# Phi moved to VectorE, a sine table to ScalarE, and a new order of the plan, in a gated mix of memory attention and a spectral filter

## The chip, the cores and the metric

One core of a Trainium2 chip runs the whole kernel in one launch. The metric is the device time of the program in microseconds, from 2048 tokens of width 640 in HBM to the output in HBM. The engines are TensorE (PE in the profile), VectorE (DVE), ScalarE (ACT), GpSimd (POOL) and SyncE (SP), which here only issues transfers.

## The reference

Two branches work on inputs of 2048 x 640 in bf16, and a gate per token mixes them. Branch A is attention with a compressive memory in 4 segments of 512 tokens, with 32 heads of width 20. Both branches get `A_x` as their x; `B_x` is not used.

```python
g = sigmoid((x * gate_w).sum(-1))
# A, for each segment s of 4, each head
phi = lambda t: where(t > 0, t + 1.0, exp(t))
p     = softmax(qs @ ks.T * 20**-0.5 + causal_mask)
a_dot = p @ vs
a_mem = (phi(qs) @ M) / (phi(qs) @ z + 1e-6)
o     = sigmoid(beta) * a_mem + (1 - sigmoid(beta)) * a_dot
M, z  = M + phi(ks).T @ vs, z + phi(ks).sum(0)
a     = concat(o) @ wo
# B
b = irfft2(rfft2(x) * (w_r + 1j * w_i))
out = g * a + (1 - g) * b
```

## The kernel before

The kernel is written as a graph of operations. `Graph.op` records each operation with the engine or the engines that may run it, what it reads and writes, a duration in the planner's own units of microseconds (`dur`) and a priority (`pr`; the lower value goes first). `Graph.schedule` then lays all operations out in time by these durations: at each step it takes, among what is ready, the operation that could start first, and by priority where several could start within 0.04 us. An operation that needs PSUM takes one of eight banks when it starts (`acq`) and gives it back with the copy that empties it (`rel`); `AHEAD` says how far in priority an operation may run ahead of the most urgent one that still needs a bank of its class. Where an operation may run on two engines, as the copies out of PSUM may on ScalarE and VectorE, the plan chooses one. `Emit` writes the instructions of each engine in the planned order, with semaphore waits between the engines. On the chip each engine then goes through its list in this fixed order; the durations in the plan no longer matter there.

The planner also imitates TensorE's clock: where it sees TensorE idle before an operation, it may put dummy matmuls there (L495), each of 512 columns, which read only `xT` and write to the bank that the operation has just been given. `WARM` holds the time from which this is done, a lower and an upper bound for the share of recent TensorE work, and the largest number of dummies in one place. `Emit.emit` writes the waits of an operation first, and then the operation's instructions, the dummies at their head.

The set-up (`tables`) computes arguments on VectorE and sines on ScalarE, for cosine and sine tables: `Df` for the transform along the width, `tab0` to `tab5` for the transform along the tokens, `Di` for the way back. The odd sine table `tab3` is made from the odd cosine table `tab2`, read backwards and multiplied with a sign for each partition (`scol`); before, this is a GpSimd instruction of 2048 columns (L822). All exponentials of the kernel are ordered behind all sines, so that ScalarE changes its function table once.

The spectral branch folds `xT` by symmetry on VectorE, multiplies with `Df` into `Z`, transforms along the tokens (`Aev`, `Bev`), filters with the weights `W` (`filter`: `X1`, `X2`, `Mt`, `Nt`, `St`, results in `FG`) and transforms back into `YT`; its start is spread by `DF0`, `DF1`, `FWD0`, `FWD1`, `INV0`, `INV1`.

The attention goes over 32 slots: 4 segments with 8 groups of 4 heads. For each 128 tokens `project` makes k, q and v (`pk`, `nq`, `vaug`), stores k and q to HBM on SP's queue (`hk`, `hq`), and computes phi of both in place; phi of q is stored too (`hp`). `fetch` reads them back transposed (`kT`, `qT`, `pqT`), also on SP's queue. `scores` multiplies them, takes the exponential on ScalarE (`ex`) and clears the upper triangle of the diagonal blocks on GpSimd (`affine_select`, L1144); `weigh` multiplies with `vaug` and with the memory `Mz`, and normalizes on VectorE. `memory_update` adds phi(k) times v. `project_out` makes 128 rows of the output: the last step of the spectral branch (`cs`, `ys`; the two additions into `ys` may run on GpSimd or VectorE), the transposes of `osb`, the product with `wo`, and the sum on VectorE (`outt`, L1215).

Phi is the part that the change touches most. Before, it is computed as max(t, 0) + min(exp(t), 1), with the exponential on ScalarE, both limits on GpSimd (L1068 and L1069) and the sum on VectorE. It runs 24 times (12 for k and 12 for q, over 128 x 640 each), and there is one buffer `ek` for the exponential, so that one phi ends before the next begins. The instructions of the helpers `ve`, `tt`, `act`, `copy` and `po` appear in the profile with the helpers' lines: L535 is a VectorE operation on two tensors, L514 a ScalarE function, L525 and L528 are copies on ScalarE and VectorE, and L497 is a matmul.

Of the kernel before, what the change touches and what calls it, by code (L numbers as in the profile page):

```python
# [6 lines left out]
ACT = mybir.ActivationFunctionType  # L7
ALU = mybir.AluOpType
# [425 lines left out]

UNITS = ((0,), (1, 3), (2,))

DF0, DF1, FWD0, FWD1, INV0, INV1, PR0, PR1 = -15.079, 0.53, -3.827, 1.2, 8.0, 0.819, -16.0, 0.105

GATE, OUT0, OUT1, YLEAD = -16.128, (14.574, 23.59, 27.761, 32.159), 0.707, 0.204

PC0, PC1 = 0.3, 0.562
NOSB = 2
NCS = 2

YENG = ("pool", "dve")

TRP, DIP = -15.053, -29.071

WARM = (24.0, 0.437, 0.837, 6)

SC0, SCP, SCU, WG0, WG1, FE0, FE1 = 0.0, 0.359, 0.076, 1.221, -0.212, 0.125, -0.026
AHEAD = 1.4


EXU = {(0,): (0, 512), (1, 3): (1024, 512), (2,): (2048, 256)}
# [11 lines left out]
class Kern(Graph):  # L467
# [40 lines left out]
            return h  # L508
        return self.op("pe", fn, r=list(r) + [self.ident.keys[0]], w=[req], dur=0.06 * n, pr=pr, acq=req if acq else None)

    def act(self, out, in_, func, r, w, n, pr, scale=1.0, bias=None, rel=None):
        def fn(e):
            kw = {} if bias is None else {"bias": bias}
            return e.activation(out(), in_(), func, scale=scale, **kw)  # L514
        o = self.op("act", fn, r=r, w=w, dur=0.05 + n * 0.000835, pr=pr, rel=rel)
        if func == ACT.Sin:
            self.sins.append(o)
        if func == ACT.Exp:
            o.after.update(self.sins)
        return o  # L520
# [160 lines left out]
    def loads(self):  # L681
        x2 = self.x2
        for i, c in enumerate((0, 3, 1, 2)):
            self.dma("sp", self.xT[:, :, c * L:(c + 1) * L], x2[c * L:(c + 1) * L, :], [], [self.xT.keys[c]], lat=4.0, transpose=True, dur=4.2, pr=-100 + i)
        self.dma("act", self.gwrow[0:5, :], self.gate_w.rearrange("(t p) -> t p", p=P), [], [self.gwrow.keys[0]], lat=3.0)
        self.dma("act", self.beta[:, :], AP(self.A_beta.tensor, self.A_beta.offset, [[0, P], [1, H]]), [], [self.beta.keys[0]], lat=3.0)
        for i, j in enumerate((1, 0, 2)):
            t, w = self.wqkv[j], (self.A_wq, self.A_wk, self.A_wv)[j]
            self.dma("act", t[:, :, :], w.rearrange("(t p) e -> p t e", p=P), [], [t.keys[0]], lat=8.0 + 2.5 * i, pr=-99 + i, dur=0.5)

        self.late = []
        for t in range(4):
            self.load_w(0, t)
        self.late.append(self.dma("sp", self.wo[:, :, :], self.A_wo.rearrange("(t p) e -> p t e", p=P), [], [self.wo.keys[0]], lat=6.0, pr=0, dur=0.5))
# [83 lines left out]
    def tables(self):  # L778
        k = lambda t: t.keys[0]
        n = [0]  # L780

        def make(dst, wkeys, prods, rk, width, mask, scale, pr, parts=None):
            a = self.arg[n[0] % 2]
            n[0] += 1
            for (o, row, c, ph, cost) in prods:
                out = a.ap(o[0], o[1])
                self.op("dve", lambda e, out=out, row=row, c=c, ph=ph: e.tensor_scalar(out, row, c, ph, ALU.mult, ALU.add), r=rk, w=[k(a)], dur=0.07 + cost * 0.00065, pr=pr)  # L787
            self.ve(lambda e: e.tensor_scalar(a[:, 0:width], a[:, 0:width], mask, None, ALU.bitwise_and), [k(a)], [k(a)], width, pr, rate=1.6)  # L788
            for (d_, off, dims) in (parts or [(dst, 0, [[1, width]])]):
                self.act(lambda d_=d_: d_, lambda off=off, dims=dims: a.ap(off, dims), ACT.Sin, [k(a), k(self.npi)], wkeys, width, pr, scale=scale, bias=self.npi[:, 0:1])  # L790

        dsc = 2 * PI / 65536.0
        ssc = 2 * PI / 4096.0
        dc, cf = self.dcol, self.colf

        for (t0, nt) in ((0, 3), (3, 2)):
            pr = []
            for t in range(t0, t0 + nt):
                for j, ph in ((0, 49152.0), (1, 0.0)):
                    pr.append((((t - t0) * 2 * HC + j * HC, [[1, HC]]), self.krow[:, :], dc[:, t:t + 1], ph, HC))  # L800
            make(self.Df.ap(t0 * 2 * HC, [[1, nt * 2 * HC]]), [k(self.Df)], pr, [k(self.krow), k(dc)], nt * 2 * HC, 65535, dsc, -40)
        self.ve(lambda e: e.memset(self.Df.ap(HC + 319, [[2 * HC, 5], [1, 2]]), 0.0), [], [k(self.Df)], 10, -40)
        er, orr = self.erow, self.orow

        def stab(i, row, c0, ph):
            t = self.tab[i]
            nt, w = t.t.shape[1], t.t.shape[2]
            pr = []
            for j in range(nt):
                pr.append(((j * w, [[1, w]]), row[:, 0:w], cf[:, c0 + j:c0 + j + 1], ph, w))  # L810
            if i == 1:

                pr.append(((0, [[512, 2], [1, 1]]), cf.ap(0, [[1, 2], [1, 1]]), 1024.0, ph, 4))
            make(t.ap(0, [[1, nt * w]]), [k(t)], pr, [k(row), k(cf)], nt * w, 4095, ssc, -38 + i)
        stab(0, er, 0, 3072.0)
        stab(1, er, 0, 2048.0)
        stab(2, orr, 0, 3072.0)

        sc, pc, t2, t3 = self.scol, self.pcol, self.tab[2], self.tab[3]
        self.ve(lambda e: e.tensor_scalar(pc[:, :], pc[:, :], 1, None, ALU.bitwise_and), [k(pc)], [k(pc)], 1, -36)  # L820
        self.ve(lambda e: e.tensor_scalar(sc[:, :], pc[:, :], -2.0, 1.0, ALU.mult, ALU.add), [k(pc)], [k(sc)], 1, -36)
        self.po(lambda e: e.tensor_scalar(t3.ap(0, [[512, 4], [1, 512]]), t2.ap(511, [[512, 4], [-1, 512]]), sc[:, 0:1], None, ALU.mult),  # L822
                [k(t2), k(sc)], [k(t3)], 2048, pr=-35)

        for i in (0, 1):
            q = Psum(1, "A")
            t = self.tab[i]
            self.tp(lambda q=q, t=t: [(AP(self.psbf.tensor, self.psbf.offset + q.bank * 1024 + 256 * c + P * j, [[8192, P], [1, P]]), t[:, j, P * c:P * c + P])
                                      for c in range(4) for j in range(2)], [k(t)], q, TRP + i, acq=True, n=8)
            self.copy(lambda i=i: self.tab[4 + i].ap(0, [[1, 1024]]), lambda q=q: AP(self.psbf.tensor, self.psbf.offset + q.bank * 1024, [[8192, P], [1, 1024]]),  # L830
                      [q], [k(self.tab[4 + i])], 1024, TRP + i, rel=q, dve=0.62)

        rk = [k(self.drow), k(dc)]
        h = self.hcol
        for part, ph in ((0, 49152.0), (1, 0.0)):
            pr = [((j * HC, [[1, HC]]), self.drow[:, :], dc[:, 5 + t:6 + t], ph, HC) for j, t in enumerate(((0, 1, 2), (2, 3, 4))[part])]
            make(self.Di.ap(3 * part * HC, [[1, 3 * HC]]), [k(self.Di)], pr, rk, 3 * HC, 65535, dsc, DIP)
            self.ve(lambda e, part=part: e.tensor_scalar(self.Di[:, 2 + part, :], self.Di[:, 2 + part, :], h[:, part:part + 1], None, ALU.mult), [k(self.Di), k(h)], [k(self.Di)], HC, DIP)
# [173 lines left out]
    def attention(self):  # L1012
# [13 lines left out]
        for n, (s, g) in enumerate(slots):  # L1026
            if n + 2 < len(slots):
                self.fetch(n + 2, *slots[n + 2], n + FE0, "kq")
            if n + 1 < len(slots):
                self.fetch(n + 1, *slots[n + 1], n + FE1, "p")  # L1030
            self.scores(n, s, g)
            for u, at in PIECES:
                if s < 3 and int(at) == g:
                    self.project(s + 1, *u, 8 * s + at)
            self.weigh(n, s, g)
            if g == 7 and s < 2:
                self.memory_update(s + 1, n + 1.6)
            if g == 7:
                for i in range(4):
                    self.project_out(s, i, OUT0[s] + OUT1 * i)  # L1040

    def project(self, s, m, i, pr):
# [20 lines left out]
        def phi(t, off, key, e_, pr):  # L1063
            v = lambda: t.ap(off, [[32, 32], [1, DH]])
            ev = lambda: e_.ap(0, [[DH, 32], [1, DH]])
            self.act(ev, v, ACT.Exp, [key], [k(e_)], D, pr)

            self.po(lambda e: e.tensor_scalar(v(), v(), 0.0, None, ALU.max), [key], [key], D, pr=pr)  # L1068
            self.po(lambda e: e.tensor_scalar(e_[:, :], e_[:, :], 1.0, None, ALU.min), [k(e_)], [k(e_)], D, pr=pr)  # L1069
            self.tt(v, v, ev, ALU.add, [key, k(e_)], [key], D, pr, rate=1.55)  # L1070
        if m == "q":
            part(self.wqkv[0], lambda: nq.ap(0, cols), nq.keys, pr)
            store("q", nq[:, :], nq.keys, pr)
# [109 lines left out]
    def project_out(self, s, i, pr):  # L1183
# [16 lines left out]
        for d0, step, n, c0, op in ((0, 1, HC, 0, ALU.add), (639, -1, 319, 1, ALU.subtract)):  # L1200
            def comb(e, d0=d0, step=step, n=n, c0=c0, op=op):
                return e.tensor_tensor(ys.ap(d0, [[step, n]]), cs.ap(c0, [[1, n]]), cs.ap(HP + c0, [[1, n]]), op)
            self.op(YENG, comb, r=[k(cs)], w=[k(ys)], dur={"pool": 0.85, "dve": 0.24}, pr=pr - YLEAD + 0.05)
        q = Psum(1, "A")
        self.tp(lambda: [(AP(self.psbf.tensor, self.psbf.offset + q.bank * 1024 + c * P, [[8192, P], [1, P]]), osb[:, i, c * P:(c + 1) * P]) for c in range(5)],
                [k(osb)], q, pr, acq=True)
# [43 lines left out]
```

## Time and profile before

| what | value |
|---|---|
| median of 3 runs | 356.12 us (351.96 to 357.1) |
| the profiled execution's own time | 356.99 us |
| its span, from the first to the last instruction | 354.9 us |
| mean granted TensorE clock | 0.918 |
| busy: TensorE, VectorE, ScalarE, GpSimd | 290.6, 270.1, 230.4, 219.5 us |
| phi on GpSimd: L1068 and L1069, 48 instructions | 89.7 us |
| causal selects on GpSimd: L1144, 192 instructions | 107.9 us |
| exponentials of the scores: L514, 192 instructions | 157.1 us |
| dummy matmuls: L495 | 20 weight loads (14 of the matmuls are in the trace) |
| DMA | 34.78 MB, mean 98 GB/s |

The page gives the busy time of each engine, the chain of work that ended last (followed back from the last instruction, at each step to what released it), and the costliest groups of instructions, each with its engine, tiles, shape, count, busy time, mean duration, and the idle time of the engine before it with what ended it. A group's line can be that of a helper, so groups are told apart by their tiles. Busy time is a sum over stages that differ: the set-up and the spectral transforms up to some 80 us, the filter and the inverse transform beside the first two segments up to some 200 us, and attention with the projections of the output from there on. Where durations of single instructions are given, they come from the same profiled execution.

### The profile page before, as it was taken

What the parts mean: (1) busy time and instruction counts of PE and PEld (TensorE: products, weight loads), DVE (VectorE), ACT (ScalarE), POOL (GpSimd) and SP (SyncE); (2) the same over time, 40 slices, a digit from 0 to 9 for tenths busy, and PEclk for the clock granted to TensorE, in tenths of its full rate; (3) what the DMA queues carried; (4) which work ended last, traced back from release to release, by engine and by line L of the source; (5) the groups of instructions that cost most, each with busy time, mean ns of one, the idle gap of its engine ahead of it and who ended that gap; (6) DMA issues with size and microseconds to landing.
All of it is one profiled execution on the core that took longest, in us unless ns stands there. A gap on an engine that the chain in (4) does not pass through costs nothing.

```text
span 354.9 us, 8311 instructions
## 1 busy us (share of the span) xinstructions
PE 290.6 (82%) x3385; PEld 185.3 (52%) x3397; DVE 270.1 (76%) x531; ACT 230.4 (65%) x307; POOL 219.5 (62%) x296
## 2 busy tenths in 40 slices
PE   0794886998498768699797789798997989999976
PEld 0473554665255435365554455475665555656444
DVE  5798687199999999689998758676665586776646
ACT  3584352688379929678678477457797567787800
POOL 9344862064988777959778679427878444454400
PEclk9999898999769969879999699899999699999769
DMA  6993362014244313226322344334556243443102
GB/s 153 322 303 97 64 132 76 0 16 118 59 100 98 125 25 77 74 65 130 91 79 73 88 121 76 108 69 139 157 115 160 76 79 86 96 83 77 35 0 76
DMA packets 74276, 34.78 MB, mean 98 GB/s; under 512 B 59902, under 2 KB 68606, under 8 KB 74238
## 3 DMA queue, kind: packets, MB, share of 16 engines
q1 hardware_dynamic: 72116, 31.78, 36.8%
q10 hardware_dynamic: 2122, 2.47, 2.2%
q8 instruction: 27, 0.44, 0.6%
q14 instruction: 11, 0.09, 0.1%
HBM read 5.92 MB, written 14.16 MB: 57 GB/s over the span
## 4 chain that ended last, share of the span: by engine, by line
PE 35%; DVE 23%; POOL 21%; ACT 12%; issue 6%; DMA 2%; SPq 0%; POOLq 0%; DVEq 0%
PE psum L497 32%; ACT ex L514 8%; POOL ek L1069 8%; POOL ex L1144 5%; DVE arg L787 4%; POOL nq L1068 4%; POOL pk L1068 4%; DMA hq<-nq 2%; DVE Nt L535 2%; DVE PQ L535 2%; PE psum L495 1%; DVE arg L788 1%; PE psum L507 1%; ACT ek L514 1%; DVE osb L535 1%
## 5 line engine op out<-in xcount | busy, mean ns | idle before, releaser
L514 ACT ACTIVATE ex<-psum 128x1024 bf16<-128x1024 f32 (+1 forms) x192 | 157.1, 890 | 38.8 <-PE psum L497 38.5
L1144 POOL TENSOR_SCALAR_AFFINE_SELECT ex<-ex 128x256 bf16<-128x256 bf16 (+1 forms) x192 | 107.9, 580 | 67.5 <-ACT ex L514 67.3
L497 PE MATMUL psum<-qT,kT 32*128 32x128 bf16 (+2 forms) x640 | 59.9, 286 | 17.6 <-DVE Aev L528 4.5
L497 PEld LDWEIGHTS psum<-qT,kT 32*128 32x128 bf16 x640 | 25.4, 95 | 55.4 <-issue 14.6
L1069 POOL TENSOR_SCALAR ek<-ek 128x640 bf16<-128x640 bf16 x24 | 45.0, 1876 | 7.0 <-ACT ek L514 6.7
L497 PE MATMUL psum<-vaug,ex 128*128 128x22 bf16 x1280 | 39.0, 173 | 4.3 <-POOL ex L1144 3.6
L497 PEld LDWEIGHTS psum<-vaug,ex 128*128 128x128 bf16 x1280 | 36.3, 97 | 9.3 <-POOL ex L1144 4.3
L497 PE MATMUL psum<-Df,fold 128*128 128x321 bf16 x160 | 26.1, 328 | 10.5 <-DVE fold L535 5.8
L497 PE MATMUL psum<-wk,xT 128*128 128x320 bf16 x160 | 27.8, 329 | 4.9 <-DMA xT<-in_A_x_dram 3.9
L497 PE MATMUL psum<-wq,xT 128*128 128x320 bf16 x160 | 25.6, 310 | 3.8 <-DVE pk L528 3.4
L1068 POOL TENSOR_SCALAR pk<-pk 128x640 bf16<-128x640 bf16 x12 | 22.4, 1871 | 8.9 <-ACT ek L514 8.3
L497 PEld LDWEIGHTS psum<-Df,fold 128*128 128x128 bf16 x160 | 16.6, 106 | 19.9 <-DVE fold L535 7.0
L497 PE MATMUL psum<-wo,oT 128*128 128x320 bf16 x160 | 25.7, 313 | 1.1 <-DVE oT L528 0.7
L497 PE MATMUL psum<-wv,xT 128*128 128x320 bf16 x160 | 25.9, 314 | 0.4 <-ACT ex L514 0.2
L1215 DVE SCALAR_TENSOR_TENSOR outt<-psum,g,ys 128x640 bf16<-128x640 f32 x16 | 14.1, 882 | 15.2 <-PE psum L497 15.0
L1068 POOL TENSOR_SCALAR nq<-nq 128x640 bf16<-128x640 bf16 x12 | 22.3, 1858 | 4.0 <-ACT ek L514 2.0
L497 PEld LDWEIGHTS psum<-wk,xT 128*128 128x128 bf16 x160 | 16.1, 106 | 13.6 <-DMA xT<-in_A_x_dram 4.0
L497 PE MATMUL psum<-Z,tab 128*128 128x321 bf16 x96 | 17.3, 335 | 5.0 <-DVE osb L535 3.9
L497 PEld LDWEIGHTS psum<-wq,xT 128*128 128x128 bf16 x160 | 15.1, 100 | 11.0 <-DVE pk L528 3.5
L497 PEld LDWEIGHTS psum<-wo,oT 128*128 128x128 bf16 x160 | 15.5, 102 | 9.4 <-DVE oT L528 1.7
L535 DVE TENSOR_TENSOR otmp<-psum,ws 128x640 bf16<-128x640 f32 x24 | 19.7, 823 | 0.7
L497 PEld LDWEIGHTS psum<-wv,xT 128*128 128x128 bf16 x160 | 15.6, 103 | 8.8 <-ACT ex L514 0.7
(142 smaller groups left out, 484.6 us busy)
## 6 DMA issues: line engine op xcount, KB each, us to landing
hk<-pk SPq DMA_DIRECT2D x16, 256.0 KB, 2.4
hq<-nq SPq DMA_DIRECT2D x16, 256.0 KB, 2.7
hp<-nq SPq DMA_DIRECT2D x12, 256.0 KB, 2.2
out_dram<-outt SPq DMA_DIRECT2D x16, 160.0 KB, 1.9
W<-in_B_w_r_dram SPq DMA_DIRECT2D x15, 80.2 KB, 2.3
W<-in_B_w_i_dram SPq DMA_DIRECT2D x15, 80.2 KB, 2.3
wk<-in_A_wk_dram ACTq DMA_DIRECT2D x1, 800.0 KB, 8.6
wq<-in_A_wq_dram ACTq DMA_DIRECT2D x1, 800.0 KB, 10.8
```

What stands on the lines that cost most here:

```text
L495: e.matmul(self.bk(req, 0, [[1, 512]]), self.xT[:, 0, 0:P], self.xT[:, 0, 0:L], start=True, stop=True)
L497: h = e.matmul(o, l, rr, start=st, stop=sp, tile_position=tp)
L507: h = e.transpose(o, i, self.ident[:, :])
L514: return e.activation(out(), in_(), func, scale=scale, **kw)
L535: return self.ve(lambda e: e.tensor_tensor(out(), a(), b(), op), r, w, n, pr, rate, rel, eng)
L787: self.op("dve", lambda e, out=out, row=row, c=c, ph=ph: e.tensor_scalar(out, row, c, ph, ALU.mult, ALU.add), r=rk, w=[k(a)], dur=0.07 + c ...
L788: self.ve(lambda e: e.tensor_scalar(a[:, 0:width], a[:, 0:width], mask, None, ALU.bitwise_and), [k(a)], [k(a)], width, pr, rate=1.6)
L1068: self.po(lambda e: e.tensor_scalar(v(), v(), 0.0, None, ALU.max), [key], [key], D, pr=pr)
L1069: self.po(lambda e: e.tensor_scalar(e_[:, :], e_[:, :], 1.0, None, ALU.min), [k(e_)], [k(e_)], D, pr=pr)
L1144: self.po(lambda e, dg=dg, nd=nd: e.affine_select(dg, dg, [[0, nd], [1, P]], ALU.is_ge, 0.0, base=0, channel_multiplier=-1), [ke], [ke], n ...
L1215: self.ve(lambda e: e.scalar_tensor_tensor(v3(ot), self.bk(q2, 0, [[512, 2], [1, HB]]), self.g[:, st:st + 1], v3(ys), ALU.mult, ALU.add), ...
```

## The change

Phi becomes max(t + 1, min(exp(t), 1)): the minimum is a VectorE instruction on the contiguous buffer `ek`, and one VectorE instruction (`scalar_tensor_tensor`) adds 1 to t and takes the maximum. GpSimd has no part in phi any more. The odd sine table is made by a ScalarE copy with a scale per partition, reading backwards as before. The constants of the plan change: the priorities of the transforms, the projections, the output and the fetches, the lead of the last spectral step (`YLEAD`), the priorities of two table steps (`TRP` for the transposed tables, `DIP` for `Di`), `WARM` and `AHEAD`. So do some durations that the planner works with: phi's steps, the arrival of the weights, and the two additions into `ys`. In the loop over slots the slot of a projection is limited to 0 to 7.

```diff
-DF0, DF1, FWD0, FWD1, INV0, INV1, PR0, PR1 = -15.079, 0.53, -3.827, 1.2, 8.0, 0.819, -16.0, 0.105
+DF0, DF1, FWD0, FWD1, INV0, INV1, PR0, PR1 = -16.909, -0.881, -2.68, 0.28, 9.813, 1.123, -15.163, 0.571
-GATE, OUT0, OUT1, YLEAD = -16.128, (14.574, 23.59, 27.761, 32.159), 0.707, 0.204
+GATE, OUT0, OUT1, YLEAD = -15.788, (15.953, 24.482, 28.405, 32.291), 0.533, 1.675
-PC0, PC1 = 0.3, 0.562
+PC0, PC1 = 0.791, 0.494
-TRP, DIP = -15.053, -29.071
+TRP, DIP = -6.184, -78.177
-WARM = (24.0, 0.437, 0.837, 6)
+WARM = (24.0, 0.445, 1.592, 14)
-SC0, SCP, SCU, WG0, WG1, FE0, FE1 = 0.0, 0.359, 0.076, 1.221, -0.212, 0.125, -0.026
-AHEAD = 1.4
+SC0, SCP, SCU, WG0, WG1, FE0, FE1 = 0.38, 0.154, -0.106, 0.784, -0.874, -0.521, -1.157
+AHEAD = 6.17
...
-    def act(self, out, in_, func, r, w, n, pr, scale=1.0, bias=None, rel=None):
+    def act(self, out, in_, func, r, w, n, pr, scale=1.0, bias=None, rel=None, rate=0.000835):
...
-        o = self.op("act", fn, r=r, w=w, dur=0.05 + n * 0.000835, pr=pr, rel=rel)
+        o = self.op("act", fn, r=r, w=w, dur=0.05 + n * rate, pr=pr, rel=rel)
...
-            self.dma("act", t[:, :, :], w.rearrange("(t p) e -> p t e", p=P), [], [t.keys[0]], lat=8.0 + 2.5 * i, pr=-99 + i, dur=0.5)
+            self.dma("act", t[:, :, :], w.rearrange("(t p) e -> p t e", p=P), [], [t.keys[0]], lat=(8.0, 11.0, 25.5)[i], pr=-99 + i, dur=0.5)
...
-        self.po(lambda e: e.tensor_scalar(t3.ap(0, [[512, 4], [1, 512]]), t2.ap(511, [[512, 4], [-1, 512]]), sc[:, 0:1], None, ALU.mult),
-                [k(t2), k(sc)], [k(t3)], 2048, pr=-35)
+        self.act(lambda: t3.ap(0, [[512, 4], [1, 512]]), lambda: t2.ap(511, [[512, 4], [-1, 512]]), ACT.Copy, [k(t2), k(sc)], [k(t3)], 2048, -35, scale=sc[:, 0:1])
...
-                if s < 3 and int(at) == g:
+                if s < 3 and min(7, max(0, int(at))) == g:
...
-            self.act(ev, v, ACT.Exp, [key], [k(e_)], D, pr)
-
-            self.po(lambda e: e.tensor_scalar(v(), v(), 0.0, None, ALU.max), [key], [key], D, pr=pr)
-            self.po(lambda e: e.tensor_scalar(e_[:, :], e_[:, :], 1.0, None, ALU.min), [k(e_)], [k(e_)], D, pr=pr)
-            self.tt(v, v, ev, ALU.add, [key, k(e_)], [key], D, pr, rate=1.55)
+            self.act(ev, v, ACT.Exp, [key], [k(e_)], D, pr, rate=0.00093)
+            self.ve(lambda e: e.tensor_scalar(e_[:, :], e_[:, :], 1.0, None, ALU.min), [k(e_)], [k(e_)], D, pr, rate=3.8)
+            self.ve(lambda e: e.scalar_tensor_tensor(v(), v(), 1.0, ev(), ALU.add, ALU.max), [key, k(e_)], [key], D, pr, rate=0.96)
...
-            self.op(YENG, comb, r=[k(cs)], w=[k(ys)], dur={"pool": 0.85, "dve": 0.24}, pr=pr - YLEAD + 0.05)
+            self.op(YENG, comb, r=[k(cs)], w=[k(ys)], dur={"pool": 0.72, "dve": 0.38}, pr=pr - YLEAD + 0.05)
```

## The prediction

> **What bounds the kernel now.** I read the busy table first, then the chain of work that ended last, then the costliest groups, then the busy time by stage, and last the timeline where the chain is thick. Busy time and chain:
>
> ```profile
> PE 290.6 (82%) x3385; PEld 185.3 (52%) x3397; DVE 270.1 (76%) x531; ACT 230.4 (65%) x307; POOL 219.5 (62%) x296
> ...
> PE 35%; DVE 23%; POOL 21%; ACT 12%; issue 6%; DMA 2%; SPq 0%; POOLq 0%; DVEq 0%
> PE psum L497 32%; ACT ex L514 8%; POOL ek L1069 8%; POOL ex L1144 5%; DVE arg L787 4%; POOL nq L1068 4%; POOL pk L1068 4%; DMA hq<-nq 2%; DVE Nt L535 2%; DVE PQ L535 2%; PE psum L495 1%; DVE arg L788 1%; PE psum L507 1%; ACT ek L514 1%; DVE
> ```
>
> No engine bounds the whole span. GpSimd is only 62% busy, yet 21% of the chain is its work, and the three phi entries (ek, nq, pk) are most of that: in the chain's finer list 7.8, 4.1 and 3.7%, or 15.6% of 354.9 us = 55.4 us. The groups behind it, with the ScalarE and VectorE ends of phi and the one big GpSimd multiplication of the set-up:
>
> ```profile
> L1069 POOL TENSOR_SCALAR ek<-ek 128x640 bf16<-128x640 bf16 x24 | 45.0, 1876 | 7.0 <-ACT ek L514 6.7
> L1068 POOL TENSOR_SCALAR pk<-pk 128x640 bf16<-128x640 bf16 x12 | 22.4, 1871 | 8.9 <-ACT ek L514 8.3
> L1068 POOL TENSOR_SCALAR nq<-nq 128x640 bf16<-128x640 bf16 x12 | 22.3, 1858 | 4.0 <-ACT ek L514 2.0
> L535 DVE TENSOR_TENSOR nq<-nq,ek 128x640 bf16<-128x640 bf16 x12 | 9.8, 813 | 11.5 <-POOL nq L1068 9.2 <-POOL ek L1069 2.3
> L535 DVE TENSOR_TENSOR pk<-pk,ek 128x640 bf16<-128x640 bf16 x12 | 6.8, 569 | 12.2 <-POOL ek L1069 11.3 <-POOL pk L1068 0.9
> L822 POOL TENSOR_SCALAR tab<-tab,scol 128x2048 bf16<-128x2048 bf16 x1 | 6.0, 6038 | 1.9 <-ACT tab L514 1.9
> ```
>
> A phi lasts about 5 to 8 us from its exponential to its sum, and there is one ek buffer, so the next exponential waits for the sum before it. The stages show who could run faster if that went (columns: stretch, its length, busy time and instructions of PE, weight loads, DVE, ACT, POOL, then clock and DMA):
>
> ```profile
> 0.00:35.00 35.00, 19.96 (x199) 14.12 (x199) 27.64 (x49) 18.21 (x20) 18.92 (x46) 1.00 0.83 221
> 35.00:56.00 21.00, 15.09 (x98) 9.67 (x98) 15.07 (x36) 9.13 (x18) 15.09 (x8) 0.92 0.48 116
> 56.00:80.00 24.00, 23.45 (x185) 15.23 (x186) 15.35 (x30) 15.30 (x25) 5.74 (x10) 0.93 0.07 7
> 80.00:140.00 60.00, 47.38 (x508) 28.64 (x507) 58.50 (x131) 42.80 (x61) 45.69 (x46) 0.86 0.34 87
> 140.00:200.00 60.00, 48.17 (x591) 29.83 (x596) 52.16 (x109) 41.93 (x57) 47.69 (x54) 0.91 0.34 85
> 200.00:280.00 80.00, 70.83 (x944) 46.36 (x942) 52.98 (x92) 57.45 (x73) 57.53 (x77) 0.93 0.46 115
> 280.00:345.00 65.00, 58.84 (x820) 36.93 (x824) 42.94 (x82) 44.76 (x56) 28.06 (x56) 0.92 0.31 66
> ```
>
> From 80 to 140 us VectorE is full (58.5 of 60), from 56 to 80 and from 200 on TensorE nearly is. So the 55.4 us can't all come back: in each stage the gain ends at the next full engine.
>
> **The change, part by part.** *phi.* Off GpSimd go 24 x 1.876 + 12 x 1.871 + 12 x 1.858 = 89.7 us. Off VectorE go the 24 sums, 9.8 + 6.8 = 16.6 us. On VectorE come 24 minima over 640 contiguous bf16 and 24 fused add-and-max. No row has such a minimum. From below, the 128x321 bf16 tensor_scalar of Di took 0.295 us at half the size; from above, 128x512 in int32 took 0.483, which by size is 0.60. I take 0.38, nearer the bf16 row: that row plus 319 more elements at half the int32 rows' slope of (1.225 - 0.684)/1024 us. For the fused one the six 128x642 bf16 scalar_tensor_tensor of the filter (L988) took 0.88 to 0.96 and outt from PSUM 0.882; I take 0.90. That is 24 x 1.28 = 30.7 us, so VectorE gains 14.1 us of work (12 to 20 by the ends). The latency of a phi falls from over 5 us to 0.74 + 0.38 + 0.90 and handovers, about 2.2 us. The minimum now waits on VectorE for ScalarE's exponential; behind it in VectorE's order stand copies out of PSUM (0.82 us each), and TensorE stands for their banks. The sum stood there for GpSimd so far, 9.2 + 2.3 + 11.3 + 0.9 = 23.7 us of idle time in the two rows above, so this wait moves and shrinks.
>
> Against this stands that VectorE is stretched beside GpSimd. Comparing each two-input VectorE instruction with the fast tenth of its own shape, 29 of them lost 12.4 us beside phi's GpSimd work and 72 lost 19.3 us beside the causal selects (L1144). The first sum vanishes, the second stays, and the 24 new pairs take their part of it (0.27 us for one hit, 72 of 360 hit, so 1.3 us for the fused ones, and as much or a little more for the minima). Net VectorE: 14.1 - 12.4 + 3 = +5 us.
>
> The worst such stretch is in the set-up:
>
> ```profile
> 24.17 6.04 POOL L822 TENSOR_SCALAR tab<-tab,scol 128x2048 bf16<-128x2048 bf16 x1 [1.87 <-ACT tab L514]
> 24.89 5.50 DVE L787 TENSOR_SCALAR arg<-drow,dcol 128x321 int32<-128x321 int32 x1
> ```
>
> The same instruction takes 0.38 us elsewhere; here it stands until GpSimd has finished. The Trainium skill (SBUF — State Buffer, Who interferes with whom) says that GpSimd and a VectorE instruction in a two-port mode, or with two SBUF inputs, exclude each other for the whole instruction. The 5.50 us agree; the two-input sums beside a 1.87 us phi instruction don't, they lost about 0.53 us at most. The rule speaks against the change, since a minimum is a two-port candidate: by it each would stand up to a whole select, 24 x 0.58 = 14 us by the mean of the selects.
>
> *The odd sine table* goes to ScalarE: 6.04 us leave GpSimd, one ScalarE copy of 2048 comes, 2.0 us by the 2048-wide sine's row (2.002). VectorE's 5.1 us of standing go, and they lie on the chain; the copy lies beside the folds. I take -5 (bounds -8, because the cosine tables of the inverse are now planned first and the switch from Sin to Exp could come sooner than 33.4 us, and +2, if the copy delays the first exponentials).
>
> *The stages.* 35 to 56 us: four phi in a row set the chain while TensorE waits for folds. VectorE's 15.1 us become about 15.1 + 4 x 0.6 - 1.5 = 16 of 21; I take -3 (0 to -5). 56 to 80: TensorE full, 0. 80 to 140: six phi, +3.5 us of VectorE work and -5.9 us of stretch beside phi: -2.5, and half a microsecond of its idle time; -3 (+3 to -6). 140 to 200: seven phi, +4 and -3.6 cancel; of 7.8 us idle on VectorE I take the 3.6 that it stood for phi's GpSimd work in the view of waits; -4 (0 to -8). 200 to 280: the eight phi here are most of the chain, but TensorE has only 9.2 us idle; I take two thirds, -6 (0 to -9). 280 on: no phi; 0.
>
> *Priorities.* Every start in the plan moves, the transposed loads and stores on SP's queue with them; SP waits 96.9 us for TensorE before transposed loads already, for rings to come free, and an earlier load cannot pass that. The two small spectral additions may go to GpSimd more often (costs 0.72 and 0.38 in place of 0.85 and 0.24); two of 32 run there now, 0.722 us each, and each moved one saves VectorE 0.36 to 0.59 after 200 us, where VectorE is not the bound: 0. The order of the rest is worth 0 to me, with +-8 us as bounds, by VectorE's idle 27 us from 200 to 280, to which spectral work can move or from which it can be missed.
>
> The new prices of wv's load and of phi's exponential, and the clamp on the projections' slots, change no instruction: 0 beside the order.
>
> *Dummy matmuls* (L495). The planner puts them where it sees TensorE idle, up to 14 in place of 6, and the upper share that stopped them (0.837) becomes 1.592, which no share reaches. But the code issues them after the waits of the operation that they precede:
>
> ```profile
> 84.99 0.38 PE L495 MATMUL psum<-xT 128*128 128x512 bf16 x1 [0.75 <-DMA W<-in_B_w_i_dram]
> ```
>
> They read only xT, yet stood for W. So each is added behind a wait instead of filling it, at 0.21 us (a second in a row makes 0.38 into 0.60), twice that at the half clock. There are 20 now. Against it stands the clock: mean 0.918, so (1 - 0.918) x 354.9 = 29 us of full-speed time are missing. The Trainium skill (TensorE: Matmul & The Clock Gate, Part 1) has the clock fall to half after an idle window of 3.4 us and rise after a busy one; by it filled gaps would save up to those 29 us. I take 40 more, 8 us of TensorE, half on the chain, against 4 us of clock: 0 (-8 to +15, more in a rival).
>
> **Sum.** 5 + 3 + 3 + 4 + 6 = 21 us off the profiled execution's 356.99 us (span 354.9, 2.1 outside): 336. That execution lies 0.9 us above the median of 356.1, so **335 us**; the stage bounds alone give 319 to 356.
>
> **Rivals.**
> 1. *The phi chain comes back nearly whole* (0.18). The 55.4 us become some 15 pairs with 0.63 us more VectorE each, 9.5 us, and the plan, priced nearer to the rows, uses TensorE's 64 us of idle time: 357 - 46 + up to 10 taken back, about 315. For it: TensorE is idle 64 us in all. Against: VectorE at 58.5 of 60.
> 2. *VectorE takes the place of GpSimd* (0.13). If minima cost 0.6 and each stands for a whole select, as the set-up's instruction stood (24 x 0.58, the selects' mean), VectorE grows 20 + 14 - 12 = 22 us, and from 80 to 200 that eats every gain; the set-up and a little late work remain: 351. Against: 200 to 345 has VectorE room.
> 3. *Slower: dummy matmuls behind waits* (0.15), on TensorE from 56 us on, where it is 80 to 98% busy. They cancel the 21 us at 100 extra (0.21 each), and from some 135 over 2% is lost. With 200 extra at half-clock share 42 to 50 us: 357 - 21 + 30, about 366. For it: no share stops them and 14 is the cap. Against: 20 now, with the cap of 6 rarely met.
> 4. That phi stays where it was can't be: the code names one engine for each.
>
> **Numbers.** The forecast, 322 to 349, has 0.54. Measurement can tell about 2% from no change, so within 2% is 349 to 363. Faster is the forecast and rival 1: 0.72; same is rival 2: 0.13; slower is rival 3: 0.15. The range 316 to 358 leaves out about a tenth on either side: most of rival 3 above, half of rival 1 below.
>
> **What would show it.** Right: GpSimd busy near 125 us with no phi rows; VectorE 262 to 280 us; minima at 0.3 to 0.6 and fused ones at 0.88 to 0.96; no VectorE instruction above 2 us; GpSimd's chain share below 10%, PE's and DVE's larger. Wrong: L495 above 120, or minima with a mean above 0.8, or VectorE over 290 us, or a first exponential later than 35 us.

## The result and the profile after

The changed kernel takes 314.7 us (median; 313.4 to 316.75) against 356.5 us before: the ratio is 0.886, with an interval of 0.878 to 0.893, or 41.8 us. The side was forecast, the size was not: 335 us was predicted with a range from 316, and the time lies just under it, where the first rival stood (about 315). Medians here are over all executions; ratios and their intervals leave out the few that lay over 1.5% above the fastest of the same kernel. The profiled execution took 315.56 us, with a span of 313.7.

The busy table and the chain of the page of the changed kernel:

```profile
PE 275.8 (88%) x3396; PEld 179.6 (57%) x3409; DVE 256.9 (82%) x544; ACT 234.5 (75%) x311; POOL 139.5 (44%) x255
...
PE 51%; DVE 30%; ACT 10%; DMA 4%; POOL 2%; issue 2%; ACTq 0%; DVEq 0%
PE psum L497 48%; ACT ex L514 7%; DVE Nt L535 3%; DMA wk<-in_A_wk_dram 3%; DVE FG L535 3%; POOL ex L1141 2%; DVE Mt L535 2%; PE psum L507 2%; DVE PQ L535 2%; PE psum L495 2%; ACT ek L514 2%; DVE St L535 1%; DVE YT L535 1%; DVE X L535 1%; DV
```

GpSimd has gone from 21% of the chain to 2%, TensorE's share has grown from 35 to 51%. TensorE's own busy time fell from 290.6 to 275.8 us though its work stayed (12 dummies more): the granted clock rose from 0.918 to 0.983, so the same matmuls ran shorter. VectorE has 13 us less, not 5 more. The groups of the new phi (columns as before: count, busy us, mean ns, idle before):

```profile
L1067 DVE SCALAR_TENSOR_TENSOR nq<-nq,ek 128x640 bf16<-128x640 bf16 x12 | 10.4, 864 | 3.8 <-DMA hq<-nq 3.7
L1067 DVE SCALAR_TENSOR_TENSOR pk<-pk,ek 128x640 bf16<-128x640 bf16 x12 | 10.3, 859 | 0.1
L1066 DVE TENSOR_SCALAR ek<-ek 128x640 bf16<-128x640 bf16 x24 | 8.3, 344 | 1.6 <-ACT ek L514 1.3
```

These come to 29.0 us (30.7 predicted), and VectorE stands 5.5 us before them, where it stood 23.7 before the old sums.

To see where the time went, the span is cut at the first exponential of each segment's scores, so that each row holds one segment's scores; the last row ends where the last exponential starts. First the kernel before, then the changed one (columns: stretch, length, then busy time of PE, weight loads, DVE, ACT, POOL, the clock, and DMA):

```profile
69.70:157.30 87.60, 70.63 (x763) 43.40 (x764) 81.14 (x173) 63.36 (x89) 66.44 (x72) 0.86 0.31 74
157.30:228.70 71.40, 59.08 (x732) 36.50 (x733) 58.22 (x113) 50.68 (x68) 55.63 (x64) 0.94 0.38 94
228.70:287.40 58.70, 53.49 (x737) 35.08 (x738) 37.43 (x67) 42.69 (x55) 37.19 (x55) 0.93 0.47 119
287.40:335.70 48.30, 44.99 (x661) 28.56 (x663) 35.35 (x67) 37.91 (x49) 24.47 (x49) 0.97 0.37 78
```

```profile
62.50:138.00 75.50, 64.19 (x733) 39.41 (x735) 71.81 (x166) 60.70 (x85) 40.59 (x52) 0.93 0.31 85
138.00:194.90 56.90, 52.57 (x692) 32.55 (x698) 55.13 (x120) 49.41 (x70) 28.53 (x48) 1.00 0.43 109
194.90:251.10 56.20, 53.81 (x759) 35.85 (x756) 41.39 (x75) 43.75 (x56) 27.59 (x52) 1.00 0.47 124
251.10:296.70 45.60, 44.70 (x679) 29.60 (x674) 34.09 (x66) 38.82 (x50) 26.65 (x53) 1.00 0.40 95
```

Of the 41 us of span, 7.2 come from what lies before the first scores (69.7 to 62.5), 12.1 from the first segment, 14.5 from the second, 2.5, 2.7 and about 2 from the rest. In the changed kernel VectorE is 95 and 97% busy in the first two segments, TensorE 96 and 98% in the last two. Before, no engine passed 83% in the second segment.

### The profile page after: what moved, and what is told of

Same layout as the page of the kernel before. It is cut to its first block, busy times and chain, and to the rows that moved or that the text cites. A ratio compares the mean times of both kernels' runs of the same rounds, so it can differ in the third digit from the quotient of the medians.

```text
span 313.7 us, 8311 instructions
## 1 busy us (share of the span) xinstructions
PE 275.8 (88%) x3396; PEld 179.6 (57%) x3409; DVE 256.9 (82%) x544; ACT 234.5 (75%) x311; POOL 139.5 (44%) x255
## 4 chain that ended last, share of the span: by engine, by line
PE 51%; DVE 30%; ACT 10%; DMA 4%; POOL 2%; issue 2%; ACTq 0%; DVEq 0%
PE psum L497 48%; ACT ex L514 7%; DVE Nt L535 3%; DMA wk<-in_A_wk_dram 3%; DVE FG L535 3%; POOL ex L1141 2%; DVE Mt L535 2%; PE psum L507 2%; DVE PQ L535 2%; PE psum L495 2%; ACT ek L514 2%; DVE St L535 1%; DVE YT L535 1%; DVE X L535 1%; DVE W L528 1%
## 5 line engine op out<-in xcount | busy, mean ns | idle before, releaser
L1141 POOL TENSOR_SCALAR_AFFINE_SELECT ex<-ex 128x256 bf16<-128x256 bf16 (+1 forms) x192 | 114.6, 604 | 101.5 <-ACT ex L514 100.4
L497 PE MATMUL psum<-qT,kT 32*128 32x256 bf16 (+2 forms) x640 | 59.4, 276 | 7.5 <-ACT ex L514 2.5
L497 PE MATMUL psum<-vaug,ex 128*128 128x22 bf16 x1280 | 41.7, 173 | 4.4 <-POOL ex L1141 2.8
L497 PE MATMUL psum<-wo,oT 128*128 128x320 bf16 x160 | 24.1, 299 | 0.3 <-ACT ex L514 0.3
L729 POOL COPY W<-W 128x4 bf16<-128x4 bf16 x8 | 5.4, 674 | 41.7 <-DVE W L528 40.2
L497 PE MATMUL psum<-Df,fold 128*128 128x321 bf16 x160 | 22.3, 300 | 0.0
L497 PEld LDWEIGHTS psum<-Df,fold 128*128 128x128 bf16 x160 | 15.6, 98 | 6.5
L525 ACT ACTIVATE Z<-psum 128x321 bf16<-128x321 f32 (+1 forms) x23 | 12.2, 533 | 7.5 <-PE psum L497 7.2
L1169 DVE RECIPROCAL rs<-psum 128x32 f32<-128x32 f32 x24 | 8.5, 353 | 10.1 <-PE psum L497 9.9
L497 PE MATMUL psum<-Di,YT 128*128 128x321 bf16 x96 | 16.0, 302 | 0.1
## 6 DMA issues: line engine op xcount, KB each, us to landing
wq<-in_A_wq_dram ACTq DMA_DIRECT2D x1, 800.0 KB, 12.1
```

The source lines that it names most:

```text
L497: h = e.matmul(o, l, rr, start=st, stop=sp, tile_position=tp)
L525: return e.activation(out(), in_(), ACT.Copy, scale=1.0 if scale is None else scale)
L729: self.po(lambda e: e.tensor_copy(W.ap(322, [[WP, 4], [1, 1]]), W.ap(1, [[WP, 4], [1, 1]])), W.keys, W.keys, 4, pr=pr)
L1141: self.po(lambda e, dg=dg, nd=nd: e.affine_select(dg, dg, [[0, nd], [1, P]], ALU.is_ge, 0.0, base=0, channel_multiplier=-1), [ke], [ke], n ...
L1169: self.ve(lambda e: e.reciprocal(rs.ap(0, [[16, 2], [1, 16]]), self.bk(q, 20, [[512, 2], [22, 16]])), [q], [k(rs)], 32, pr + WG1, rate=0.16)
```

## The experiments

Each is compared with the kernel before on the same chip. "The order before" means: the plan is made with the old work, prices and constants, and only then are the named instructions exchanged, so that every other instruction keeps its place on its engine. Where a kernel is "planned", the planner laid everything out anew.

**1. The moved work in the old order.** For phi:

```diff
+        for a, b, c, fn in self.phis:      # GpSimd's maximum, its minimum, VectorE's sum
+            order.remove(a); order.remove(b)
+            order.insert(order.index(c), b)
+            b.chosen = "dve"
+            c.fn = fn                      # scalar_tensor_tensor: (t + 1) max e
+            c.deps = (c.deps | a.deps) - {a}
```

> The order of the kernel before is kept on every engine; only phi's instructions change: the maximum goes, the minimum goes from GpSimd to VectorE just ahead of the sum, and the sum becomes the fused add-and-max. Theory W (the move of the work carries the gain, in any order): about 325 us, clock above 0.96. Theory O (the new order of the plan carries most of it): about 343 us, clock near 0.93. Theory V (VectorE takes GpSimd's place and the old order cannot move its work): about 352.

> The order before is kept; only the odd sine table is made by a ScalarE copy at its old place in the plan, in place of GpSimd. All theories: VectorE's 5.5 us instruction falls to 0.4 us. If the stall was on the path that sets the end, 351 us; if the four phi in a row behind it set the start of the scores anyway, 355.

> The order before is kept, with phi on VectorE and the odd sine table on ScalarE together: all the moved work of the change, none of its new order. Theory W: 318 us. Theory O: 337 us. Theory V: 347 us.

Phi alone: 327.6 us, ratio 0.922 (0.912 to 0.932). The sine table alone: 351.0, ratio 0.987 (0.982 to 0.992), with VectorE's 5.5 us instruction gone. Both: 325.6, ratio 0.918 (0.910 to 0.927). So theory W holds for 30 of the 42 us, short of its numbers. The table's gain of about 4.5 us shrinks to 1 or 2 once phi has moved, which is within the scatter of these runs. TensorE's busy time, the same instructions on the same list, is 278.5 us with phi alone and 277.1 with both, where it was 290.6.

**2. The new order with phi put back on GpSimd.** In the changed kernel's order VectorE's minimum is exchanged for both limits on GpSimd and the fused form for a plain sum.

> The order of the changed kernel is kept, with the odd sine table on ScalarE, but both limits of phi go back to GpSimd, one after the other, at the place of VectorE's minimum, and the sum is a plain sum. Theory W: 350 us or more, as GpSimd's 90 us come back onto the chain. Theory O: about 330 us. In an order that was planned without them they may cost more than they did before: above 356 would say that the new order needs the move.

385.4 us, ratio 1.086 (1.077 to 1.096): slower than the kernel before by 30 us. The page's chain has GpSimd at 21% again. The new order needs the moved work; in it phi on GpSimd costs 70 us.

**3. Constants and work, planned.** One kernel has the new constants and prices with the old work, the other the new work and prices with the old constants.

> The work of the kernel before (phi's limits and the odd sine table on GpSimd), planned with the constants and the prices of the changed kernel. If the constants are good by themselves: about 345 us. If they only suit the moved work, as the run with phi put back on GpSimd in the new order (385 us) suggests: 356 to 385 us.

> The moved work of the changed kernel, planned anew with the new prices but with the old constants (priorities, lead, bounds of the dummies). The moved work in the old order took 325.6 us, the changed kernel 314.7. If the new prices make the plan: 315 to 318. If the constants do: 322 to 330. If the plan is a matter of luck within some per cent: anything from 315 to 340.

348.6 us (ratio 0.974, 0.964 to 0.985) and 327.4 (0.920, 0.912 to 0.929). With the two known corners: the constants bring about 7 us with the old work (5 to 13 by the interval) and 12.7 with the new, the work 28 with the old constants and 34 with the new. The new prices alone made no better plan than the old order with exchanged instructions (325.6).

**4. Dummies and the clock.** All dummies are left out of the changed kernel's order.

```diff
+        for o in order:
+            o.spare = 0
```

> The changed kernel in its own order, with all dummy matmuls left out. Theory K (the dummies keep TensorE's clock up, and the clock is where the time came from): clock near 0.95 and 322 us or more. Theory N (they stand behind waits and the clock stays up because long waits are gone): clock 0.97 to 0.985 and 310 to 315 us.

315.2 us, ratio 0.886 (0.879 to 0.892): the time of the changed kernel, as theory N has it. But the clock fell to between 0.957 and 0.962 in the four runs, below N's guess, where it was 0.972 to 0.983 with them: the 32 dummies do hold it up, and it buys nothing. TensorE's busy time is 277.4 us without them and 275.8 with them, so what they add and what the faster clock saves nearly cancel. What a higher clock would bring without that cost is not shown.

**5. Why phi on GpSimd cost 28 us: five runs in the old order.** The first moves only the sums of the kernel before back in VectorE's list, phi staying on GpSimd.

> The kernel before, phi still on GpSimd, but each sum of phi stands up to 8 VectorE instructions later in VectorE's list, with what depends on it behind it; everything else keeps its order. Theory H (VectorE standing for GpSimd's limits, the copies out of PSUM behind it, and TensorE standing for their banks are what phi on GpSimd costs): about 340 us, clock above 0.94, the waits of VectorE for phi's GpSimd steps under 8 us in place of 23.7. Theory G (it is GpSimd's own time and the latency of phi): 354 to 360, since both stay.

354.4 us, ratio 1.000 (0.996 to 1.005): theory H's 340 us did not come. VectorE's standing did go: its waits for phi's GpSimd steps fell from 23.7 to 3.8 us in all. Other waits grew, as the views of waits show (who waits, for whom, us in total, times, longest), first of the kernel before, then of this run:

```profile
ACT ek L514 <- DVE pk L535: 20.3, 8, 4.6
...
POOL pk L1068 <- ACT ek L514: 8.3, 4, 4.1
...
POOL ek L1069 <- ACT ek L514: 6.7, 4, 3.7
...
PE psum L497 <- POOL ex L1144: 3.6, 4, 2.3
...
POOL nq L1068 <- ACT ek L514: 2.0, 2, 1.8
```

```profile
ACT ek L514 <- DVE pk L535: 16.1, 10, 3.8
POOL pk L1088 <- ACT ek L514: 14.2, 5, 5.1
...
POOL ek L1089 <- ACT ek L514: 13.3, 9, 3.8
PE psum L497 <- POOL ex L1165: 12.2, 9, 3.1
...
POOL nq L1088 <- ACT ek L514: 12.1, 5, 3.8
```

GpSimd's waits for phi's exponentials grew from 17.0 to 39.6 us in the three rows, and TensorE's for the selects, which stand behind phi in GpSimd's list, from 3.6 to 12.2. But the edit does two things at once. It takes VectorE's standing away, and it makes each phi end later: 8.7 us on average after its exponential starts, where it was 6.1. The run with late phi below shows that lateness of that size costs many microseconds, so the two may have cancelled. What VectorE's standing costs by itself this run does not show.

The next three start from phi on VectorE in the old order (327.6 us) and put back one part of the cost each: phi ends late, with GpSimd free; or GpSimd is busy again at the old places (more than before with six instructions for a limit, about as before with four), with phi free of it.

```diff
+        # late: each fused sum, and what depends on it, up to 8 VectorE instructions later
+                    order[i:j + 1] = rest + dep
```

```diff
+        # scratch: at the place of each limit, n instructions that nobody waits for
+                return e.tensor_scalar(sa[:, :], self.ones[:, 0:64], 0.0, None, ALU.max)
```

> Phi on VectorE in the old order, but each minimum stays and each fused add-and-max stands up to 8 VectorE instructions later, with what depends on it behind it: phi ends some 3 to 4 us later, about when it did with GpSimd, while GpSimd stays free. Theory L (late phi is what cost): 340 us or more. Theory Q (GpSimd's list is): 326 to 331.

> Phi on VectorE in the old order as in the run that took 327.6 us, but each of the 48 limits leaves on GpSimd, at its old place and behind the same waits, six short instructions over 64 columns of a scratch tile, for which nobody waits; together they should keep GpSimd busy about as long as the limit did (1.9 us). Theory L (what cost the time is that phi passes through GpSimd, so that the sum and all behind it came late): 327 to 333 us. Theory Q (what cost it is GpSimd's list: the causal selects stand behind the limits, and TensorE and ScalarE's buffers behind the selects): 340 to 352.

> As the run with short scratch instructions on GpSimd, with four in place of six for each limit: about 2.1 us each, 100 us in all against the 90 us of the limits (six took 3.1 us each, 150 us, and 368 us in all). If GpSimd's list costs by its length: 0.27 us for each us from 327.6 to 368, so about 353. If it costs from a point on only, when the selects become late: 330 to 345.

Late phi: 341.9 us, ratio 0.966 (0.958 to 0.974); a phi lasts 8.3 us on average from the start of its exponential to its end, against 5.2 with phi on VectorE and 6.1 before. So each phi is 3.1 us later here, where GpSimd had made it 0.8 us later: lateness costs time, but the 14.3 us are for a dose almost four times the true one. The scratch instructions, six to a limit: 368.4 us, ratio 1.041 (1.027 to 1.055). Four to a limit: 339.0, ratio 0.951 (0.945 to 0.957). The groups of the six and of the four, and TensorE's waits for the selects with six and with four:

```profile
L1095 POOL TENSOR_SCALAR scr<-ones 128x64 bf16<-128x64 bf16 x288 | 130.8, 454 | 30.1 <-ACT ek L514 8.3
```

```profile
L1095 POOL TENSOR_SCALAR scr<-ones 128x64 bf16<-128x64 bf16 x192 | 92.1, 480 | 27.2 <-ACT ek L514 10.6 <-issue 2.0 <-DMA hq<-nq 0.6
```

```profile
PE psum L497 <- POOL ex L1174: 36.1, 16, 6.7
```

```profile
PE psum L497 <- POOL ex L1174: 8.7, 6, 3.3
```

Four come to 92.1 us of work, close to the limits' 89.7, so GpSimd's list at its true load costs 11.4 us, though nobody waits for the scratch results. The list does not cost by its length: 92 us cost 11, and 39 more cost 29, because then GpSimd (250 of 364 us busy) makes TensorE stand for the selects.

That leaves 16.6 of the 28 us. VectorE does not explain them by its load, for it is equally busy in the kernel before and with phi moved (270.1 us). They lie between the true lateness of phi, VectorE's standing of 23.7 us, and what the parts do together; no run separates these. An estimate from the three runs: 14.3 us for 3.1 us of lateness is 4.6 each; then the true 0.8 us would cost about 4, the 2.6 us in the run with late sums about 12, and VectorE's standing, which that run took away at no gain, would be worth about as much. 11.4, 4 and 12 come near 28, but the estimate supposes that lateness costs alike in both runs.

The fifth leaves out both limits on every engine:

> The order before is kept and both limits of phi are left out on every engine, so that phi is computed as t + exp(t); VectorE's plain sum stays at its place. It is the run with phi on VectorE in the old order (327.6 us) without the 12 us that the minimum and the fused form add to VectorE. If VectorE takes GpSimd's place as the bound: 316 to 320 us. If VectorE's added work lies in its idle time: 324 to 327.

318.9 us, ratio 0.903 (0.896 to 0.909), 8.7 us less than with phi on VectorE. More than the expected 12 us went off VectorE: phi's instructions there come to 12.8 us in place of 30.4, and VectorE is busy 253.9 us in place of 270.1. So about half of it comes off the time, though a phi is also 1.0 us shorter here (4.2 us). VectorE does take part of GpSimd's place as the bound.

**6. Which constants.** Each kernel is the changed one, planned with one group of old constants.

> The changed kernel planned with the old priorities of the transforms, first projections and table steps (DF, FWD, INV, PR, TRP, DIP); all else new. The constants together are worth 12.7 us with the new work (327.4 against 314.7). If the transforms' new places carry it: 322 to 328. If the attention's and the output's places and the lead do: 312 to 318.

> The changed kernel planned with the old places of scores, weights, fetches and later projections (SC0 to FE1, PC0, PC1), all else new, AHEAD too. If these carry the constants' 12.7 us: 322 to 328. If the transforms' places do (5 us by the run with the old ones): 315 to 320.

> The changed kernel planned with the old places of the gate and of the output projections and the old lead of the last spectral step (GATE, OUT, YLEAD), all else new. The old constants lost their time in the last segment (55 us there against 46), where the output projections are spread; if their places carry it: 322 to 327. If not: 313 to 318.

319.9 us (0.904, 0.897 to 0.912), 333.0 (0.935, 0.928 to 0.941) and 322.6 (0.905, 0.899 to 0.912). The three losses against 314.7 are 5, 18 and 8 us, 31 in all, where all old constants together lose only 12.7; with the old places of the attention alone it is slower than with all old ones (327.4). The losses do not add, so the groups depend on each other, and no single one carries the gain. The last one's loss falls mostly into the last segment, as expected of it (50.9 us from its first exponential to its last, against 45.6).

**7. Less work for VectorE in the new order.** Phi is also min(max(t + 1, 1), exp(t)), since exp(t) is never under t + 1.

```diff
-  tensor_scalar(ek, ek, min 1);  scalar_tensor_tensor(t, (t + 1) max ek)
+  tensor_scalar(t, t, add 1, max 1);  tensor_tensor(t, t, ek, min)
```

> The changed kernel in its own order, with phi as min(max(t + 1, 1), exp(t)): one VectorE tensor_scalar with two operations on t, then a plain minimum of two tensors, in place of the minimum on the exponential and the fused form. The plain form should take 0.48 to 0.5 us in place of 0.86, the other 0.32 to 0.5: VectorE loses 4 to 9 us. Taking 12 us off VectorE in the old order gave 8.7 us. So 308 to 312 us where VectorE's work still counts, 314 where the new order has room for it.

> The changed kernel once more, unaltered, to stand beside the next one on the same chip: 313 to 316 us.

> The changed kernel in its own order with phi as min(max(t + 1, 1), exp(t)), once more beside the changed kernel. If the 2 us between 312.6 and 314.7 are real: 2 to 4 us under it here too. If VectorE's work no longer counts in the new order: within 1 us of it.

First 312.6 us, ratio 0.876 (0.870 to 0.882). Side by side: the changed kernel 314.6 (0.887, 0.882 to 0.892), this one 311.0 (0.877, 0.872 to 0.883). So it is the fastest of all by 3.6 us, though the two intervals touch. Its VectorE rows in the first of these runs:

```profile
L1075 DVE TENSOR_TENSOR nq<-nq,ek 128x640 bf16<-128x640 bf16 x12 | 7.0, 585 | 0.4
L1075 DVE TENSOR_TENSOR pk<-pk,ek 128x640 bf16<-128x640 bf16 x12 | 6.8, 569 | 0.4
L1075 DVE TENSOR_SCALAR nq<-nq 128x640 bf16<-128x640 bf16 x12 | 4.5, 372 | 4.7 <-DMA hq<-nq 4.7
L1075 DVE TENSOR_SCALAR pk<-pk 128x640 bf16<-128x640 bf16 x12 | 3.8, 314 | 1.6 <-ACT ek L514 1.5
```

22.1 us instead of 29.0. Side by side VectorE's whole busy time is 252.4 us against 256.3, and the time falls by about as much, which fits a kernel whose first two segments are VectorE's. But GpSimd is busy less too, 128.3 us against 140.4, most of it in the selects (106.1 against 115.6), and no run tells the two apart.

## Why the prediction was wrong in size

**Right.** The prices: minimum 0.344 us (0.38 predicted), fused form 0.86 (0.90). The sine table: 5 us predicted, 4.5 measured alone, though only 1 to 2 once phi had moved. The set-up and the first phi: 8 us predicted, 7.2 in the changed kernel, 9.1 with the same work in the old order (its first scores start at 60.6 us). The dummies: 0 predicted, 0.4 measured between with and without. VectorE's stretch beside phi's GpSimd work went; beside the selects it hardly changed (20.7 us before and 20.1 after, counting losses over 0.06 us by the prediction's comparison).

**Off beside the sum.** VectorE has 13 us less, where 5 more were predicted. The set-up's stall of 5 us is one part (the sum had counted it as path only). The small spectral additions are another: ten of 32 run on GpSimd now, two before, and VectorE's share of them fell from 14.5 to 9.1 us. With these and slower selects (114.6 us, 107.9 before) GpSimd is busy 139.5 us, where near 125 was given as a sign. In the sum itself the bounds of the stages and the table add up to 320 and 361 us, not 319 and 356; the phi counted by stage are 25, there are 24; and of VectorE's standing for phi's GpSimd work from 140 to 200 us it took the largest row (3.6 us), the three rows have 5.7.

**Wrong, first step: "in each stage the gain ends at the next full engine".** For phi the stages gave 3 + 3 + 4 + 6 = 16 us; the old order with phi moved gave 28. Cut at the first exponentials as above, the profile of that run reads:

```profile
63.90:146.30 82.40, 67.98 (x761) 41.68 (x764) 78.74 (x178) 62.84 (x89) 33.84 (x56) 0.92 0.33 80
146.30:211.50 65.20, 58.45 (x740) 36.42 (x740) 58.74 (x123) 50.22 (x69) 27.29 (x48) 0.95 0.41 101
211.50:263.00 51.50, 49.65 (x731) 33.14 (x728) 38.73 (x71) 42.28 (x54) 23.16 (x47) 1.00 0.54 137
263.00:310.60 47.60, 44.19 (x667) 28.58 (x665) 35.41 (x68) 37.90 (x49) 24.56 (x49) 1.00 0.37 79
```

Beside the rows of the kernel before, 5.8 us went ahead of the first scores, 5.2, 6.2 and 7.2 in the first three segments, 0.7 in the last and 1.7 behind it (27 in all, since the profiled execution took 330.1 us). Two readings of the sum did not hold. In the third segment TensorE was busy 53.5 us before, and the segment now takes 51.5: the busy time that was read as a floor (9.2 us idle from 200 to 280) holds matmuls at the half clock. There the clock rose from 0.93 to 1.00; over the span the same list took TensorE 290.6 us before, with 58 us at the half clock, and 278.5 with phi moved, with 27. In the second segment VectorE's idle time fell from 13.2 to 6.5 us and in the first from 6.5 to 3.7, where the sum gave back 3.6 and half a microsecond in its stages there.

The price of GpSimd was sought in VectorE's 23.7 us of standing and in VectorE's stretch. What the runs show in its place is GpSimd's list ahead of the selects, 11.4 us, for which the sum had no term. How the other 16.6 us divide between VectorE's standing and the lateness of phi stays open. The latency of a phi fell less than the prediction had it: from 6.1 to 5.2 us, where about 2.2 was expected.

**Wrong, second step: the order at 0 +- 8.** It is worth 10.9 us (325.6 to 314.7), just beyond its bound. Beside the old order with both moves, the first two segments are 6.5 and 8.7 us shorter in the changed kernel, the third is 4.7 longer and the last 2 shorter. Fixed stages hid it: VectorE was full in the first segment before (81.1 of 87.6 us), with phi moved (78.7 of 82.4) and after (71.8 of 75.5), which suggests that the segment's length follows VectorE's work in it; the new order holds 7 us less of it there than the old order with phi moved, and fills VectorE to 97% in the next. The bound was taken from VectorE's idle time after 200 us and left out that of the second segment (13.2 us before, 1.8 after). Which of the constants do it stays open: exchanged one group at a time they don't add.

**Rivals.** The first was the nearest in its number, in part by luck: of its 46 us for phi 28 came, and the order made up most of the rest. Its doubt (VectorE) was in part right: with VectorE 16 us less busy, 8.7 us more would have come. The second would have had each minimum stand for a whole select; the longest took 0.75 us, and the mean lies 0.03 us over the median of 0.32. The third needed 100 dummies; there are 32 in all. The prediction's estimate of 14 us by the rule of the Trainium skill (SBUF — State Buffer, Who interferes with whom) was for every minimum meeting a select from its start; the 24 minima here took 24 x 0.025 us, 0.6, more than at their median.

## What to carry to other kernels

What an engine costs can be read neither from its share of the chain (55 us for phi here) nor from its waiters' idle time (23.7 us): moving the work gave 28. Price its list (who stands behind each long instruction), the lateness of its results and the standing of its waiters apart, with edits that change one of them only. A full engine in a stage is a limit only for that stage's present work; before taking it as a floor, ask whether work can leave the stage, and whether TensorE's busy time there was at full clock. A plan and the work it was made for belong together: in the new order the old work was 30 us slower than in its own.

## What the runs showed of the hardware

Short GpSimd instructions are dear: 64 columns of bf16 took 0.45 to 0.48 us each, nearly as much as a causal select of 256 columns (0.486 us before). On VectorE the limit of 640 columns took 0.344 us, on GpSimd 1.86 to 1.88. The fused form with two SBUF tensors ran at 0.86 us for 640 columns, where a plain two-tensor minimum takes 0.49 at best and a tensor_scalar with two operations on rows of 20 out of 32 columns 0.31 to 0.37: here the fused form saved nothing. And a mean clock raised from between 0.957 and 0.962 to between 0.972 and 0.983 by dummy matmuls left the time where it was (315.2 and 314.7 us).
